# Linear attention feeding an ELU expert layer, one core: the first batch's queries and the first expert chunk cut into token halves, with a new order of the work

## The chip, the core and the metric

The kernel runs on one core of a Trainium2 chip. The core has five engines with a queue each: TensorE (PE, matrix products and transposes), VectorE (DVE), ScalarE (ACT), GpSimd (POOL) and SyncE (SP, which here only starts transfers). Products land in PSUM, which has eight banks. The metric is the time of one launch in microseconds (us), the median over several runs.

## The reference

For eight batches of eight heads with 576 tokens of 64 values, `q` and `k` go through a feature map: a product with `w_phi` (64 x 128), less the largest absolute value of the row, then the exponential of it and of its negative. Linear attention follows, and its output, heads joined to 512 values a token, goes through two products with an ELU between them.

```python
def phi(x):
    proj = np.einsum('bhsd,df->bhsf', x, w_phi)
    proj = proj - np.max(np.abs(proj), axis=-1, keepdims=True)
    return np.concatenate([np.exp(proj), np.exp(-proj)], axis=-1)
q_p, k_p = (phi(q), phi(k))
kv = np.einsum('bhsf,bhsd->bhfd', k_p, v)
z = np.sum(k_p, axis=2)
num = np.einsum('bhsf,bhfd->bhsd', q_p, kv)
den = np.einsum('bhsf,bhf->bhs', q_p, z)[..., None] + 1e-06
x = (num / den)            # then (4608 tokens) x (512 values)
h = x @ w_in               # 512 -> 2048
g = np.where(h > 0.0, h, np.exp(np.minimum(h, 0.0)) - 1.0)
out = g @ w_out            # 2048 -> 512
```

## The kernel before

**Tiles.** The attention goes by quads: quad i is four heads of batch i // 2, so there are 16. Each sequence of 576 tokens is four tiles of 128 and a tail of 64; the tails of two heads share a tile. The expert layer goes by chunks of 512 tokens: chunk b is the 512 main tokens of batch b and needs quads 2b and 2b + 1 both, since each gives half of the 512 values; chunk 8 is all the tails.

**A quad** (`plan_quad`), with the names that stand in the profile:
- keys and queries are transposed, for the first five quads by PE through PSUM (`tr`, and `trt` for tails; copied to `kT` and `qT` by DVE or ACT), later by transposing transfers on SP's queue;
- the feature products: `pk` (keys, and also queries in token-major form, for the maxima) and `pq` (queries in feature-major form);
- maxima by DVE (`m_k`, `m_q`), exponentials by ACT (`EK` with its tails `EKt`, `Eq` with its tails `Eqt`), the row scales from the maxima by ACT (`em` for keys, `w` for queries);
- the values times the key scales by POOL (`vs`), then `pkv` on PE and its copy `kv`;
- the outputs `pn` and `pnt` (tails) on PE, weighed with `w` and added by DVE into `tot`, a divide (`den`, `rec`), and the product `x`, by DVE for quads 0 and 1 and by POOL later;
- `x` transposed into `xT`, for the first four quads by PE and a copy, later by a transfer.

**A chunk** (`plan_chunk`): 16 feature tiles; for each four matmuls of 512 columns into one bank (`ph`), the exponential by ACT (`e_sb`), minus one by POOL (`u_sb`), and the ELU by DVE (`gT`), which frees the bank. Then for each of four token tiles 16 matmuls (`po`), a copy (`o_sb`) and a store.

**Order.** `Planner` lists all of this once, as operations with a cost for each engine that may take them, and plays it through in its own model of time: at each moment an engine takes, of the operations that can start, the one with the lowest rank. The ranks are a table written into the file (`RANKS`). What comes out is a fixed order of instructions for each engine; on the chip each engine runs its list in order and waits at semaphores. PSUM banks are given out by the same play: at most four `ph` and two `po` banks at once, and six for the attention once the first `ph` has begun. While PE stands idle in the model's first 60 us, matmuls of zeros into a spare bank (`fill`) are put into the gap. Transfers of inputs and weights are started from POOL's list (and `v` from batch 2 on from SP's), so they stand in line with POOL's arithmetic.

The waits of an output tile on the `x` of the quad before and the fill rule are these lines:

```python
[o, w, *quads.get(i - 1, {}).get("x", [])],
...
if e == "PE" and 0.0 < free[e] and now < self.FILL_UNTIL and banks:
    n = int(0.5 * (now - free[e]) / self.FILL)
    if n:
        if filled not in banks:
            filled = min(banks, key=banks.get)
        self.fill(filled, n)
```

Of the kernel before, what the change touches and what calls it, by code (L numbers as in the profile page):

```python
# [34 lines left out]
    "0E0H0I0O0Q0F0J0L1T1R2Q1U2X2k1S0K2n333B2W2a3R2OHR2Y3X4b1i0z0G3s3Y0y0n3S0p0r3V0s0q"  # L35
    "3U0w0o3W0x1M1N1Q0+0v3h2g2c2b2d2e2f0X0D0A0S0U11100Z3M3O1X1c2628491K1Z1Y1v0a070b0C"
    "Ai0Y05Ah0V047k0j007m0k01Ag0W061I1F1q6A4f1+3D7A2N2B6U9m4Z2U5R6W4k1j1A181h1P191o1C"
    "1B151716090u13120t1V1W2t2i2z2r2o2s2q0d0f0g1x1z1u1y1f02032J2H2I2L4A1e1O1D2K7y1d7i"
    "2x41366w466x39483A0-4U34824T7d9G2Z3v3E4N3q3Q524H2V3F407N74AF8g2h6-4C8W8z6m3Z6D8h"
    "7P2T9B14683f42575n4I449s5o5KC14w583JC64q5d6bCy4hAj7ID35y7K1ECN5v6d08Bl676Y4xBi5g"  # L40
    "5S4yDF5w4V4uBf4v6J6t6oBU3l9H8d8v986y6MAl6B8Y9ABc4D6TBXBZ7T80Dl2v6a0B1a692m3d3z4c"
    "72201n1t1J1p1r1G1w241H1l1m1L232925274B473K3L3N3H3T3P3I0c2-314O4Q4M530P323k4J4L55"
    "4K0i354X4a500m544e3w3r3m4i4oC7C52j434E2D4YB-4d4jBpD50N0M4m6NBwB63c6f1g1b4g2R813y"
    "0l4SC05C5A3n3u593o4+4-3x5B7583213+1s2271733i3a5M3b2M2P2S2C8b8a5W5V5s5T2A8X8Z6l6n"
    "6k6h0R30454W5r6H1-5F7+5z9K9T60A+Cb5ZCLBL64DKBo5aCs9U7H9v9w6j66AxA-6SBa8E7c9PE4EI"
    "CX6G6q9-8u788L6z5t7G4GA2CZ9L5iF8Cf9uAV5IDo8j95EPDh9XASEpEc9z8IF66e8F7wEi8T9D6PBN"
    "8RAIBQDx3eAYC89FL8BYBK6OGOEQ9RHMEa9yABBO9JEgDpAHExEs9IFlA0927o7W8xGwAD9SAJD2ChEW"
    "AM2+2u2w2y0T0h2l5699C42G5O6i7x4l655q7b7e5+7q7l5x7J7S5u7L7MCQ5L5P5Q5N7X7t9x6L6s6F"
    "6p6E6I3-5-625U5b5X5c519O9Q79776v764PDH5j5h6c6RBd6XAe4r9oEy5l9t5k7F9W634n8G9a7R9N"
    "5e614s4t7f7n973t3G0e5f5YBSAXA3AaA8A5BEBIAWAwAGAEBk8H8A8B879p9rGdEHEDEAGJEFGH5pD8"  # L50
    "DBATARAUAP6VFVFWBgCwBjBh5m90BH9lCdAAE37QDXECHwGNEBHIHyA1HlGGEEGMHzBJL7GCDZFpFoAO"
    "AQMz4FH68eBFFzDn84OHCpKE9cM5ApDQ9jLhDDKpAbOmGEFI8UL0BMGyGuDdW6DjWGCPB7AsDVFOCVB9"
    "7DFN8tE-EZ7uE58kG49gJjANK2CiVXDPEnGhWID0ACC3BTCnBzDrCMHaBRVVF+DgE7CmCuOdEMDbEKEN"
    "I5BAGKDCKvEtK5D4GR2p37383C888Q2F6+3p7O3j9VCY856r9b868N8y8K8O9Z8M898+7a8J7p7r7s7v"
    "DsD-DyDm9EE1Dz70DuDaCACGCECI6Q8S8PD7D6D9DA8D8-9493CJEGCoE9Bn91GFGPA9LMJY8wG6H17U"
    "GxIZ7CG+GT2EG9GABCEX1k4p4R6u7E7jHeC9CKHS8sCHHnBuCCHYCBBmHABBCtCTCRB+C2E+B1AkB4Af"
    "B2BG7YHhHjF2FMF4FL7VHqHtC-BsC+Bq7ZLrCWCaFKCx6ZCv6CB39d7zBDA79CBW8c8fLf9i9eB57-8m"
    "8VAqAvEUHmCeOqEjByCDK7F3NPFEOYGIOsDfW19+N4DWWMTLEmAmVxTGAdEJJUPnJ2KKMvLsFCG7EdE0"
    "G5HcCcHQJKH-H5DY6KImFYEYFSFTFaHkGnGLFFF-HpDcIcHUJfHbEwK4EkG2L1ItIsNYESIFI-IxJhGr"
    "F9IKJVIPJ0UbFPIeJrJTGqPRH43g8o4z8nALAK7g7hDq8CCg96MHOZOcMLLGIhLaIwJWLdJaOhGbCzCO"  # L60
    "BrD1JuLEKkKVKdJIKuL4KZCFNQNVO9O4LVLOCrONOUMbMkMYMm8l5J9h9fMuDRG8DSHGGBHLFxG1HOFd"
    "GDHKFwG0HPFvIlE2KbFQH0H2I3ER6gAZ7B9MBVCjJZWNWQJMWKWSJXWLWRJcWJW7WU5H5E5G5DW9W8TI"
    "WVV1V0THTEWZBPBtBvJoJpJvJsAtGZGXWDWCWAWFDtWHWPWOJkIkEVDeHsI0AoAzI1AnAyEq9kB8IjBe"
    "8rGfBbAuK3JqJnElFAH8NgKnPLFrOfLwMMHiJPEvP2H3O-KRPFGtO7JCPDHBIEGlJdMAIpI9MQLnGgH+"
    "OiLmGvIzNfLjIiOBMcLiPkHgN2LUPoNqIULqPbLZORLxPhMaKCMIQuI+NkNNOvKWN5KaLWNZNcHVMPIa"
    "L5NdNaK9HfKSVlLoQfNEKGKQQTPuQLRVJ8Gj8pNJ8qFtFuG3HCLyMTFHHoGWFnFkGQFhFeGaFcFmGUFb"
# [252 lines left out]
def kernel(  # L319
# [10 lines left out]
    nc = tc.nc  # L330
# [987 lines left out]
```

## Time and profile before

| what | value |
|---|---|
| time, median of 4 runs | 369.94 us (368.76 to 371.3) |
| the profiled execution: time and span | 368.76 us, 367.0 us |
| granted TensorE clock | 1.000 |
| read from memory, written | 36.77 MB, 9.44 MB |
| first `ph` matmul | 47.56 us |
| last PE instruction ends | about 363.2 us |
| fills | 179 |

Shares of busy time are averages over stages with different limits. For one stage, the busy time by stretches and the time line are read. In a time line line stand the start, the duration (from the first start to the last end of a merged run), the engine, the line of the kernel, the operation, output <- input, the shape, the count, and in brackets how long the engine was idle before it and what ended that. Durations of PE overlap, because matmuls are pipelined; the step from one start to the next is what one costs in a row. In the stretches, after each engine's busy time stands its count of instructions, and at the end the granted clock, the mean share of the 16 DMA engines and GB/s.

### The profile page before, as it was taken

The page shows a single profiled execution, that of the slowest core. Times are in us where ns is not written, and L with a number is a line of the kernel's source. Part 1 is how long each engine was busy: PE and PEld are TensorE (multiplying, and loading weights), DVE is VectorE, ACT ScalarE, POOL GpSimd, SP SyncE. Part 2 cuts the span into 40 slices and gives each one's busy share as a digit, 9 for nine tenths or more (in the row PEclk, how much of TensorE's full clock was granted, in tenths as well). Part 3 has the DMA queues.
Part 4 walks back from the last instruction along what each step waited for, and adds up shares of the span by engine and source line. Part 5 has one row for each costly group of instructions (what it writes and reads, how often), then busy time and mean ns, then how long its engine had stood idle before and what let it go on. Part 6 is the DMA issues. An engine that isn't in the chain of part 4 may idle for free.

```text
span 367.0 us, 8937 instructions
## 1 busy us (share of the span) xinstructions
PE 350.3 (95%) x3355; PEld 194.6 (53%) x3403; DVE 270.7 (74%) x568; ACT 268.3 (73%) x595; POOL 234.1 (64%) x333
## 2 busy tenths in 40 slices
PE   7887899999999999999999999999999999999995
PEld 6666655655555554455554554565446444444444
DVE  5898999888988878875777889799968751655120
ACT  2999996899898877995669979877787623555321
POOL 8895878769795687487649573947593742545210
PEclk9999999999999999999999999999999999999999
DMA  7999999991869989578855128583210113000113
GB/s 134 238 238 205 197 198 165 175 159 51 172 142 113 129 208 193 143 144 118 102 96 153 31 40 192 149 191 67 57 63 30 35 37 109 4 29 28 59 29 86
DMA packets 86651, 43.18 MB, mean 118 GB/s; under 512 B 55632, under 2 KB 80592, under 8 KB 86608
## 3 DMA queue, kind: packets, MB, share of 16 engines
q1 hardware_dynamic: 57360, 26.36, 33.2%
q0 software_dynamic: 28848, 15.73, 30.9%
q8 instruction: 26, 0.43, 0.5%
q10 hardware_dynamic: 400, 0.52, 0.4%
q14 instruction: 17, 0.14, 0.2%
HBM read 36.77 MB, written 9.44 MB: 126 GB/s over the span
## 4 chain that ended last, share of the span: by engine, by line
PE 74%; ACT 7%; POOL 5%; DMA 4%; DVE 4%; issue 3%; SPq 1%; POOLq 0%; DVEq 0%; ACTq 0%
PE po L1128 30%; PE ph L1062 27%; PE pk L608 4%; PE pkv L828 4%; PE pn L881 3%; POOL vs L713 3%; ACT EK L659 2%; DMA v_b<-in_v_dram 2%; ACT Eq L796 2%; DMA xT<-x 1%; PE pq L746 1%; ACT EKt L659 1%; DMA k_b<-in_k_dram 1%; POOL u_sb L1078 1%; POOL x L959 1%
## 5 line engine op out<-in xcount | busy, mean ns | idle before, releaser
L1078 POOL TENSOR_SCALAR u_sb<-e_sb 128x512 bf16<-128x512 f32 x144 | 88.1, 617 | 74.2 <-ACT e_sb L1074 67.2
L1128 PE MATMUL po<-w_out_sb,gT 128*128 128x512 bf16 (+1 forms) x570 | 132.7, 373 | 1.6 <-issue 1.0
L1085 DVE SCALAR_TENSOR_TENSOR gT<-u_sb,ph 128x512 bf16<-128x512 bf16 x144 | 96.7, 681 | 46.7 <-POOL u_sb L1078 46.1
L1062 PE MATMUL ph<-xT,w_in_sb 128*128 128x512 bf16 x486 | 120.0, 379 | 1.9 <-DVE gT L1085 0.4
L1074 ACT ACTIVATE e_sb<-ph 128x512 f32<-128x512 f32 x144 | 86.1, 609 | 40.5 <-PE ph L1062 36.6
L1128 PEld LDWEIGHTS <-gT 128*128 128x128 bf16 x592 | 54.4, 98 | 57.5 <-issue 2.9
L1062 PEld LDWEIGHTS <-w_in_sb 128*128 128x128 bf16 x576 | 53.0, 98 | 60.1 <-issue 4.1
L713 POOL TENSOR_TENSOR vs<-v_b,em 128x512 bf16<-128x512 f32 (+1 forms) x96 | 77.9, 840 | 1.0 <-DMA v_b<-in_v_dram 0.9
L659 ACT ACTIVATE EK<-pk 128x512 bf16<-128x512 f32 x128 | 67.2, 622 | 12.3 <-PE pk L608 12.2
L796 ACT ACTIVATE Eq<-pq 128x512 bf16<-128x512 f32 x128 | 68.3, 623 | 6.4 <-PE pq L746 6.1
L626 DVE TENSOR_REDUCE m_q<-pk 128x4 f32<-128x512 f32 (+1 forms) x80 | 47.4, 626 | 9.5 <-PE pk L608 8.2
L626 DVE TENSOR_REDUCE m_k<-pk 128x4 f32<-128x512 f32 (+1 forms) x80 | 47.5, 628 | 8.9 <-PE pk L608 5.4
L959 POOL TENSOR_TENSOR x<-tot,rec 128x576 bf16<-128x576 f32 x28 | 31.7, 1151 | 18.8 <-DVE rec L955 18.6
L1151 ACT COPY o_sb<-po 128x512 f32<-128x512 f32 (+1 forms) x23 | 13.1, 568 | 30.1 <-PE po L1128 29.8
L916 DVE TENSOR_TENSOR tot<-pn,w 128x260 f32<-128x260 f32 x64 | 26.4, 421 | 2.2 <-PE pn L881 1.7
L881 PEld LDWEIGHTS <-Eq 128*128 128x128 bf16 x512 | 22.2, 97 | 8.9 <-issue 0.3
L922 DVE TENSOR_TENSOR tot<-tot,pn 128x260 f32<-128x260 f32 x64 | 25.9, 418 | 0.4
L828 PE MATMUL pkv<-vs,EK 128*128 128x65 bf16 x512 | 24.5, 194 | 1.2 <-POOL vs L713 0.9
L828 PEld LDWEIGHTS <-EK 128*128 128x128 bf16 x512 | 22.2, 98 | 6.3 <-issue 2.0
L881 PE MATMUL pn<-kv,Eq 128*128 128x65 bf16 x512 | 25.1, 194 | 0.1
L659 ACT ACTIVATE EKt<-pk 64x256 bf16<-64x256 f32 x64 | 22.9, 378 | 1.7 <-PE pk L590 1.1
L828 PE MATMUL pkv<-vs,EKt 128*128 128x65 bf16 x128 | 21.2, 193 | 0.8 <-POOL vs L713 0.8
(73 smaller groups left out, 289.3 us busy)
## 6 DMA issues: line engine op xcount, KB each, us to landing
out_dram<-o_sb SPq DMA_DIRECT2D x32, 256.0 KB, 2.6
v_b<-in_v_dram SPq DMA_DIRECT2D x6, 1024.0 KB, 6.4
k_b<-in_k_dram POOLq DMA_DIRECT2D x7, 512.0 KB, 7.6
q_b<-in_q_dram POOLq DMA_DIRECT2D x7, 512.0 KB, 11.3
w_in_sb<-in_moe_w_in_dram POOLq DMA_DIRECT2D x2, 1024.0 KB, 18.2
w_out_sb<-in_moe_w_out_dram POOLq DMA_DIRECT2D x4, 512.0 KB, 16.9
v_b<-in_v_dram SPq DMA_DIRECT2D x32, 32.0 KB, 5.2
v_b<-in_v_dram POOLq DMA_DIRECT2D x2, 512.0 KB, 9.5
```

The costliest lines, as they stand in the source:

```text
L626: nc.vector.tensor_reduce(dst, src, axis=AX.X, op=ALU.max, apply_absolute_value=True)
L659: nc.scalar.activation(EK()[:, 2 * c + par, sg, :] if c < 2 else EKt[r, s, sg, :], bank.tile[r, 0:n, :].rearrange("p a b -> p (a b)"), ACT ...
L713: nc.gpsimd.tensor_tensor(st["vs"][:, sg].rearrange("p (c n) d -> p c n d", c=2)[:, :, r, 0:D], kqv[b, 2][:, o:o + 2 * n * D].rearrange("p ...
L796: nc.scalar.activation(dst, src, ACT.Exp, scale=1.0 - 2.0 * sg)
L828: nc.tensor.matmul(pkv[:, c, sg, :], st["EK"][:, 2 * s + t % 2, sg, (2 * c + t // 2) * F:(2 * c + t // 2 + 1) * F,] if t < NT else EKt[:, ...
L881: nc.tensor.matmul(pt[:, t, :], st["Eq"][:, par, s, sg, o:o + P], st["kv"][:, s, c, sg, :], start=True, stop=True,)
L959: (nc.vector if e == "DVE" else nc.gpsimd).tensor_tensor(tile("x", work, [P, NS, 2, D], BF16)[:, :, c, :], tot[:, r, 0:D], st["rec"][:, r, ...
L1062: nc.tensor.matmul(ph, w_in_sb[:, ct, jt * P:(jt + 1) * P], xTs[ch][:, ct, :] if ch < B else xT_tail[:, ct // 2, :, ct % 2, :], start=(ct ...
L1074: nc.scalar.activation(t["e"], bank.tile, ACT.Exp)
L1078: nc.gpsimd.tensor_scalar(t["u"], t["e"], -1.0, 1.0, op0=ALU.add, op1=ALU.mult)
L1085: nc.vector.scalar_tensor_tensor(gTs[ch][:, jt, :], t["u"], 0.0, bank.tile, op0=ALU.min, op1=ALU.max)
L1128: nc.tensor.matmul(bank.tile, gTs[ch][:, jt, tt * P:(tt + 1) * P], w_out_sb[:, jt, o0:o1], start=(jt == 0), stop=(jt == N_JT - 1),)
```

## The change

For batch 0 (quads 0 and 1):
- the two query groups of a quad are no longer the head pairs but the token pairs: group c takes tiles c, c + 2, c + 4, c + 6 of `qT` (a strided read), that is both head pairs for half the tokens. The outputs, weights `w`, divides, products `x`, transposes and copies into `xT` follow by halves (and tails by themselves), each waiting only for its half.

For chunk 0:
- a `ph` bank holds two feature tiles of 256 tokens instead of one of 512. The first half of the matmuls of a bank needs only quad 0's half of `xT`, the second only quad 1's; all of the first token half comes before the second. `po` of the first two token tiles needs only the first half's `gT`.

For the planner:
- fills go only into a bank that has been free as long as PE, and are counted from the later of the two; 41 fills stand at the start instead of 30; the list of ranks is new throughout, so the order of every engine changes, and of the loads too: the first transfer is of `q` and not of `k`.

The core of the diff (the new `half_` functions hold the same arithmetic as the old ones on half the tokens):

```diff
-                    n = int(0.5 * (now - free[e]) / self.FILL)
-                    if n:
-                        if filled not in banks:
-                            filled = min(banks, key=banks.get)
+                    if filled not in banks or banks[filled] > free[e]:
+                        filled = min(banks, key=banks.get)
+                    n = int(0.5 * (now - max(free[e], banks[filled])) / self.FILL)
+                    if n > 0:
                         self.fill(filled, n)
...
+        halves = b == 0
...
-                project_halves(1, c, pair)
+                blocks = slice(c, 8, 2) if halves else slice(4 * c, 4 * c + 4)
+                project_halves(1, range(8)[blocks], pair)
...
-        w = add({"ACT": 0.12}, weights, m_q, key=-3.0)
+        if halves:
+            w_ops = [
+                add({"ACT": 0.12}, lambda e, tp=tp: weights_of(e, tp), m_qs[tp], key=-3.0)
+                for tp in range(3)
+            ]
+        else:
+            w_ops = [add({"ACT": 0.12}, weights, m_q, key=-3.0)] * 3
...
+            def half_outputs(e, tp=s, s=c, pair=pair):
+                for sg in range(2):
+                    pt = psum(pair[sg], [P, NT, D1], FP32, f"pn{sg}")
+                    for c in range(2):
+                        for par in range(2):
+                            o = (2 * s + c) * P
+                            nc.tensor.matmul(
+                                pt[:, 2 * c + par, :],
+                                st["Eq"][:, par, tp, sg, o:o + P],
+                                st["kv"][:, s, c, sg, :],
+                                start=True,
+                                stop=True,
+                            )
...
-            copies = kv_copies if hh == 4 else [kv_copies[s]]
-            exps = Eq_ops[s]
+            copies = kv_copies if hh == 4 else [kv_copies[c if halves else s]]
+            exps, w = Eq_ops[s], w_ops[s]
+            last = quads.get(i - 1, {})
+            last_x = last["x_ops"][s] if i == 1 else last.get("x", [])
...
-                [o, w, *quads.get(i - 1, {}).get("x", [])],
+                [o, w, *last_x],
...
+            for tp in range(3):
+                div = add(
+                    {"DVE": 0.3 if tp < 2 else 0.25},
+                    lambda e, tp=tp: divide_half(e, tp),
+                    tot_ops[tp],
+                    key=-9.0,
+                )
+                for c in range(2 if tp < 2 else 1):
+                    x_ops[tp].append(
+                        add(
+                            {"DVE": 0.36 if tp < 2 else 0.2},
+                            lambda e, tp=tp, c=c: x_half(e, tp, c),
...
-        for jt in range(N_JT):
+        for step in range(N_JT):
+            hf, jt = divmod(2 * step, N_JT) if ch == 0 else (0, step)
...
+            def mm1_half(e, g, hf=hf, jt=jt, bank=bank):
+                if g == 0:
+                    psum(bank, [P, 2, CHUNK // 2], FP32, "ph")
+                for j in range(2):
+                    for ct in (2 * g, 2 * g + 1):
+                        nc.tensor.matmul(
+                            bank.tile[:, j, :],
+                            w_in_sb[:, ct, (jt + j) * P:(jt + j + 1) * P],
+                            xTs[ch][:, ct, hf * CHUNK // 2:(hf + 1) * CHUNK // 2],
+                            start=(j == 0 and ct == 0),
+                            stop=(j == 1 and ct == N_CT - 1),
+                        )
...
+            if ch == 0:
+                for g in range(2):
+                    o = add(
+                        {"PE": 0.44},
+                        lambda e, g=g, f=mm1_half: f(e, g),
+                        [quads[g]["xT"][hf], landed["w_in", jt // 8]]
+                        + ([o] if g else []),
...
-                    [g_ops[jt] for jt in jts]
+                    [
+                        g_ops[jt if n_half == 1 else tt // 2 * 8 + jt // 2]
+                        for jt in jts[::n_half]
+                    ]
...
-    fill(7, 30)
+    fill(7, 41)
```

## The prediction

> **What bounds the kernel now.** I read the page's first two parts first, then the busy time by stretches, then the time line of the first 60 us engine by engine.
>
> ```profile
> PE 350.3 (95%) x3355; PEld 194.6 (53%) x3403; DVE 270.7 (74%) x568; ACT 268.3 (73%) x595; POOL 234.1 (64%) x333
> ...
> PE   7887899999999999999999999999999999999995
> ...
> DVE  5898999888988878875777889799968751655120
> ACT  2999996899898877995669979877787623555321
> ```
>
> TensorE (PE) is the bound of the whole, but the first five slices are thinner, and there ACT and DVE are as full as PE. The stretches before and after the first expert matmul say more:
>
> ```profile
> 0.00:47.56 47.56, 39.22 (x633) 31.53 (x634) 39.26 (x89) 39.34 (x97) 37.84 (x54) 1.00 1.23 202
> 47.56:60.00 12.44, 12.34 (x109) 6.34 (x108) 11.88 (x26) 10.86 (x24) 9.85 (x16) 1.00 1.41 174
> 60.00:363.30 303.30, 298.73 (x2621) 156.71 (x2665) 219.52 (x456) 217.72 (x475) 186.36 (x264) 1.00 0.54 103
> ```
>
> From 47.56 us PE idles 4.7 us in all. Before that its 39.2 busy us are pipelined durations, with 179 fills that compute nothing. Counted by the step from one start to the next, PE's own work there is 80 transposes x 0.0565 + 18 tail transposes x 0.075 + 112 narrow `pk` x 0.0345 + 8 wide `pk` x 0.108 + 12 `pq` x 0.155 + 8 tail `pq` x 0.055 + 216 matmuls of 65 columns x 0.0315 = 19.7 us. So 28 us of the ramp are not PE's. Only there can this change gain much, and every us by which PE reaches the same work sooner is a us of the total, as long as nothing stops PE later.
>
> ```profile
> 32.19 1.28 PE L1281 MATMUL fill<-zeros 128*128 128x128 bf16 x20 [1.65 <-DVE m_k L626]
> 34.32 0.61 PE L1011 MATMUL tr<-ident,x 128*128 128x128 bf16 x8
> ...
> 44.44 0.19 PE L828 MATMUL pkv<-vs,EKt 128*128 128x65 bf16 x1 [0.78 <-POOL vs L713]
> ...
> 45.91 0.61 PE L1011 MATMUL tr<-ident,x 128*128 128x128 bf16 x8
> ...
> 47.56 1.02 PE L1062 MATMUL ph<-xT,w_in_sb 128*128 128x512 bf16 x3
> ```
>
> The gate of the first expert matmul is the second transpose of `x` (quad 1, 45.91), and in front of it PE stands in order behind quad 2's `pkv`, which waits for GpSimd's `vs`. Quad 1's `x` itself was ready at 44.1:
>
> ```profile
> 13.79 3.54 ACT L659 ACTIVATE EK<-pk 128x512 bf16<-128x512 f32 x7 [0.31 <-PE pk L608]
> ...
> 43.32 0.80 DVE L959 TENSOR_TENSOR x<-tot,rec 128x576 bf16<-128x576 f32 x1
> ...
> 59.14 0.60 ACT L1074 ACTIVATE e_sb<-ph 128x512 f32<-128x512 f32 x1 [1.17 <-PE ph L1062]
> ```
>
> Seven exponentials in 3.54 us give ACT's step, 0.483. Until 59.14 ACT has hardly a gap.
>
> **The change part by part.** All sums are made on the profiled execution: 368.76 us, of which 367.0 are span; the median of the runs is 369.94, 1.2 higher.
>
> *When does the expert flow start?* In the instruction lists of the two programs I look for the point at which the changed PE has done as much of its own work as the old one at 47.56. That is the second half of the first `ph` tile: before it lie 84 transposes (4.7), 17 tail transposes (1.3), 88 + 7 `pk` (3.0 + 0.8), 10 + 6 `pq` (1.6 + 0.3), 200 narrow matmuls (6.3) and 16 half `ph` of 256 columns at half of 0.216 (1.7): 19.7 us as well. It needs ACT's copy of quad 1's first half of `xT`. Three chains lead there:
> - ACT: up to that copy 44 exponentials x 0.483, 16 `EKt` x 0.33, 4 `Eqt` x 0.265, 12 small ones x 0.11, 3 `kv` x 0.27, 5 tail copies x 0.16, 2 copies of 1024 x 0.91, 2 half copies x 0.483 = 33.3 us. It starts at 8.4 (8.2 now). Without idle time that is 41.7. The old list reached 33.5 us of work at 43.1 with 1.4 idle, and 38.4 at 48.8 with 2.2 idle. Ends: 41.8 and 44.0; I take 1.3 idle, the nearest row: 43.0.
> - DVE: 29.8 us of work up to quad 1's first half of `x` (22 reductions x 0.60, 14 `tot` steps, 7 large copies, the rest small), from 6.8: 36.6. The old list had 32.5 us up to its `x` and 4.7 idle. With as much, 41.3; transposes 0.45 and copy 0.5: 42.3.
> - POOL: quad 2's scales come after 26.0 us of ACT (35.2 with 0.8 idle), six `vs` take 4.8 (the row at 23.85), `pkv` 0.6, transposes 0.45, copy 0.5: 41.6.
>
> So 43.0 against 47.56: 4.5 us earlier, with the queue order that put `pkv` in front still there but ending sooner.
>
> *What halves cost.* Queries by token halves change no count of exponentials or reductions. For the two quads the divides become 6 of each kind instead of 2, the `x` products 10 instead of 4, the DVE copies of `xT` 2 instead of 1. The divide's two lines are
>
> ```profile
> 29.06 0.19 DVE L954 TENSOR_REDUCE den<-tot 128x18 f32<-128x36 f32 x1
> 29.29 0.27 DVE L955 RECIPROCAL rec<-den 128x18 f32<-128x18 f32 x1
> ```
>
> By starts, `tot` of 260 elements steps 0.335 and of 130 elements 0.20, so one more instruction costs 0.065 plus its elements; 15 more cost 1.0 us at least, and 2.2 us with the divides at 0.42 each, which I take. It is inside the 29.8. DVE is not the last of the three chains, so it costs nothing there while those 0.7 us of slack hold; without them it costs up to 2.2. [...] ACT gains four `w` (0.44) and a split copy (0.06), inside the 33.3.
>
> *The first four tiles.* From the start of flow PE has 4.5 us of work until `po` needs the fourth pair's `gT`: 47.5. DVE has 7.5 us from quad 1's first `x` (40.8) to that `gT`, 4 x 0.595 of it the ELUs: 48.3. PE waits about 0.8; with the first `gT` also freeing the bank for the fifth `ph`, I take 1.0 (ends 0 and 2.5, if DVE idles as it did). Behind PE's wait stand `ph` 5 and quad 3's `pk`. For the next four pairs ACT has 10.4 us to the last exponential (53.4), POOL 0.58 and DVE 0.6 behind it: 54.6, while PE gets there at about 56.4. No wait.
>
> *Fills.* 129 instead of 179. The old ones waited 1.65 us for a bank at 32.19 and 0.5 at 23.47; that goes, but mostly into the waits for ACT and DVE already counted, so nothing for itself. The 11 more at the start end at about 0.99 + 41 x 0.11 = 5.5, before the first data at 5.76: free. Granted clock is 1.00 in every stretch, with idle gaps up to 1.65 us. [...]
>
> *Loads.* Half the expert's input weights (`w_in`, second half) move behind quad 0's `vs` on POOL:
>
> ```profile
> L385 POOL DMA_DIRECT2D w_in_sb<-in_moe_w_in_dram x1: 778/778/778, 21.0 to 21.0; - x1
> ...
> DMA to landing us min/median/max: 19.4/19.4/19.4
> ```
>
> The new issue comes after second scales at 18.7, 4.8 of `vs` and the issue itself: 24.4, landing 43.8; the fifth pair asks at about 46. Covered by 2 us, beyond that one for one. On SP the first output store now stands ahead of quad 5's query transposes and the next `v`: `v` is issued at about 62.7 instead of 57.0 and lands 10.8 later, at 73.5; quad 4's `vs`, at 79.2 now, would ask at 75.7. Covered too, and its keys are not the next chunk's gate.
>
> *Sum.* 4.5 - 1.0 = 3.5 us. After 60 us both programs hold the same work, and chunk order is alike; I add nothing for the new ranks there and leave 1 us either way. 368.76 - 3.5 = 365.3 for a profiled execution, 369.94 - 3.5 = 366.4 for the median. Ends: 41.8 with no stall and 0.6 better later, 363.6; 44.0 with 2.5 of stall and 1 us worse later, 369.8.
>
> **Rivals.** *Given back* (no change): DVE is the true limit of the ramp. Up to the reciprocal of quad 2 the lists hold 49.25 us of DVE work after and 49.28 before, with 9 and 10 ELUs in it. If DVE idles 6.6 us again, that reciprocal stays at 62.5, and all that is left is what PE has done by then: about 36 us against 34.7, less what it waits later, 0.7 net: 369.2. For it: DVE is 95% busy from 47.56 to 60. Against: its old gaps were waits for PE and POOL in other places. *Weights late* (slower): the second half of `w_in` lands after 46, and PE, in order, stops at the fifth pair. Four POOL waits before DMA issues add to 5.3 us in the old ramp; if all fell ahead of this issue, and 0.5 MB more in front of it took 2.5 us at 0.206 MB/us, it would land at 51.6: 5.6 us of stall, 2.1 us slower, 372.0. It is slower than before from a landing at 49.5. Against: the loads that those issues wait for are earlier ones. *Fills or halves not in force*: excluded, the program's lists show both.
>
> **How the numbers follow.** The forecast 0.62, given back 0.25, weights late 0.13. About 0.5% (1.85 us) is what a measurement of this kernel can tell from no change; the forecast's own range (363.6 to 369.8) crosses that bound at its upper end, and I count that part with "given back". The range reaches from 363.6 to 371.2, into the third case, and leaves out about 2 in 10.
>
> **What would show it.** Right: `xT` copy of quad 1's first half by ACT ending near 43, a first `po` near 47, the reciprocal of quad 2 near 59 to 60, PE idle after 60 us below 6. Wrong: first `po` after 51 (weights, in the DMA line of `w_in`), DVE idle over 6 us before quad 2's reciprocal, or PE waits after 60 us that were not there.

## The result, and the profile after

The changed kernel takes 371.81 us (median of 43 runs, 369.56 to 374.17), the kernel before in the same runs 370.28 (64 runs): ratio 1.0042, 95% interval 1.0031 to 1.0053. The forecast was 366.4, in a range that ended at 371.2. The change is slower by about 1.5 us, which is still inside the 0.5% that I had set as "no change", but it lost where I had counted 3.5 us won.

The first two parts of the page of the changed kernel, the same lines as before and the clock:

```profile
PE 350.2 (95%) x3369; PEld 200.7 (54%) x3417; DVE 276.5 (75%) x583; ACT 269.3 (73%) x600; POOL 232.7 (63%) x333
...
PE   7766899999999999999999999999999999999995
...
DVE  5869899897989989786887987689988763533500
ACT  2995899899998897996679796998984553544411
...
PEclk9986799999999999999999999999999999999999
```

PE's first five slices read 77668 instead of 78878, and the clock, which was 9 throughout, falls to 8, 6 and 7 in the third to fifth. By stretches, cut at the point that the prediction worked with (the `ph` run at which PE has done what it had done at 47.56 before):

```profile
0.00:49.80 49.80, 37.42 (x553) 31.16 (x554) 40.12 (x87) 36.24 (x89) 35.31 (x52) 0.86 1.24 206
49.80:60.00 10.20, 9.79 (x98) 6.83 (x97) 9.99 (x25) 9.26 (x22) 5.20 (x8) 1.00 1.23 141
60.00:366.70 306.70, 303.00 (x2724) 162.72 (x2769) 226.37 (x473) 223.44 (x490) 192.23 (x273) 1.00 0.53 102
```

The point lies at 49.80, 2.2 us later than before, where 43.0 was predicted. From it to the end of the span it is 320.6 us against 319.4, so 1.2 us more, where the prediction had 1.0. 2.2 + 1.2 = 3.4 is the whole difference of the two spans (370.4 and 367.0). The medians differ by 1.5 only: the profiled execution of the kernel before, 368.76, is the fastest of its 64 and lies 1.5 under their median, that of the changed kernel, 372.22, lies 0.4 above its own. Measured on these two executions, as the prediction's sums were, all that went wrong lies ahead of the point.

The time line there, all engines, has one line that does not belong (the first group of each line is start and duration):

```profile
30.22 0.17 DVE L1051 RECIPROCAL rec<-den 128x2 f32<-128x2 f32 x1
...
30.40 3.06 POOL L724 TENSOR_TENSOR vs<-v_b,em 128x512 bf16<-128x512 f32 x3
...
30.62 3.00 DVE L1069 TENSOR_TENSOR x<-tot,rec 128x128 bf16<-128x128 f32 x1
33.40 0.94 POOL L411 DMA_DIRECT2D q_b<-in_q_dram  x1
...
33.68 0.29 PE L1140 MATMUL trt<-ident,x 128*128 128x128 bf16 x1 [2.76 <-DVE x L1069]
...
34.00 0.27 ACT L1148 COPY xT_tail<-trt 128x128 bf16<-128x128 bf16 x1 [2.78 <-PE trt L1140]
```

A product of 128 elements, 0.28 us where no `vs` runs (at 34.22 in the run e1 below), is on DVE for 3.00 us. It ends 0.2 us after the third of three `vs` on GpSimd. PE stands 2.76 us for it, and ACT 2.78 us behind PE. Busy time hides this: DVE counts as busy, and is even busier than before (75% against 74%).

### The profile page after: what moved, and what is told of

Same layout as the page of the kernel before. It is cut to its first block, busy times and chain, and to the rows that moved or that the text cites. A ratio compares the mean times of both kernels' runs of the same rounds, so it can differ in the third digit from the quotient of the medians.

```text
span 370.4 us, 8987 instructions
## 1 busy us (share of the span) xinstructions
PE 350.2 (95%) x3369; PEld 200.7 (54%) x3417; DVE 276.5 (75%) x583; ACT 269.3 (73%) x600; POOL 232.7 (63%) x333
## 4 chain that ended last, share of the span: by engine, by line
PE 71%; DVE 9%; POOL 8%; DMA 4%; issue 4%; ACT 3%; POOLq 0%; ACTq 0%
PE po L1338 31%; PE ph L1236 21%; PE pkv L858 5%; PE pk L609 4%; PE pn L912 3%; POOL u_sb L1268 3%; PE ph L1251 3%; DMA t_b<-in_k_dram 2%; POOL vs L724 2%; DVE x L1069 2%; DVE gT L1280 2%; DMA out_dram<-o_sb 2%; POOL x L1030 2%; PE pq L760 1%; DVE m_k L637 1%
## 5 line engine op out<-in xcount | busy, mean ns | idle before, releaser
L1264 ACT ACTIVATE e_sb<-ph 128x512 f32<-128x512 f32 x144 | 86.5, 612 | 40.1 <-PE ph L1236 37.1
L1236 PE MATMUL ph<-xT,w_in_sb 128*128 128x512 bf16 x426 | 104.0, 379 | 1.2
L1236 PEld LDWEIGHTS <-w_in_sb 128*128 128x128 bf16 x512 | 47.7, 98 | 52.6 <-issue 1.5
L670 ACT ACTIVATE EK<-pk 128x512 bf16<-128x512 f32 x128 | 68.2, 634 | 2.4 <-PE pk L609 1.6
L858 PEld LDWEIGHTS <-EK 128*128 128x128 bf16 x512 | 23.6, 101 | 7.6 <-ACT Eq L811 2.6
L858 PE MATMUL pkv<-vs,EK 128*128 128x65 bf16 x512 | 25.5, 199 | 2.3 <-ACT Eq L811 2.1
L971 DVE TENSOR_TENSOR tot<-pn,w 128x260 f32<-128x260 f32 x56 | 23.0, 422 | 5.5 <-PE pn L912 5.0
L912 PEld LDWEIGHTS <-Eq 128*128 128x128 bf16 x448 | 19.1, 97 | 7.5
L977 DVE TENSOR_TENSOR tot<-tot,pn 128x260 f32<-128x260 f32 x56 | 22.7, 418 | 0.4
L858 PE MATMUL pkv<-vs,EKt 128*128 128x65 bf16 x128 | 22.2, 198 | 0.0
L912 PE MATMUL pn<-kv,Eq 128*128 128x65 bf16 x448 | 21.1, 194 | 0.1
```

Source lines behind the costliest of these rows:

```text
L670: nc.scalar.activation(EK()[:, 2 * c + par, sg, :] if c < 2 else EKt[r, s, sg, :], bank.tile[r, 0:n, :].rearrange("p a b -> p (a b)"), ACT ...
L858: nc.tensor.matmul(pkv[:, c, sg, :], st["EK"][:, 2 * s + t % 2, sg, (2 * c + t // 2) * F:(2 * c + t // 2 + 1) * F,] if t < NT else EKt[:, ...
L912: nc.tensor.matmul(pt[:, t, :], st["Eq"][:, par, s, sg, o:o + P], st["kv"][:, s, c, sg, :], start=True, stop=True,)
L1236: nc.tensor.matmul(ph, w_in_sb[:, ct, jt * P:(jt + 1) * P], xTs[ch][:, ct, :] if ch < B else xT_tail[:, ct // 2, :, ct % 2, :], start=(ct ...
L1264: nc.scalar.activation(t["e"], flat(bank.tile), ACT.Exp)
```

## The experiments

Three theories. *Port*: DVE products and sums of two operands in SBUF (where the kernel keeps its tiles that are not PSUM banks) wait while GpSimd runs `vs`; the name is my guess at the cause, which no run shows. *Clock*: fewer fills let the granted clock fall (0.61 from 30 to 40 us), and PE's slow matmuls make the ramp late. *Count*: the 15 more DVE instructions by themselves. The table shows for each run the longest wait found on DVE (the duration of the instruction that has it), the granted clock from 20 to 30 and 30 to 40 us, the point, the rest of the span after it, and the median with its ratio to the kernel before on the same chip.

| kernel | longest on DVE, us | clock | point | rest | median | ratio |
|---|---|---|---|---|---|---|
| changed | `x` 3.00 | 0.83, 0.61 | 49.80 | 320.6 | 371.81 | 1.0042 |
| e1 old fills | `den` 2.73 | 0.83, 1.00 | 49.43 | 321.6 | 372.64 | 1.0064 |
| e2 tail of `x` on ACT | `den` 3.31 | 0.83, 0.59 | 49.44 | 320.8 | 371.48 | 1.0018 |
| e3 both | `den` 2.52 | 0.83, 0.83 | 51.36 | 320.7 | 372.67 | 1.0077 |
| e5 e2 and `den` by reduction | `x` 2.48 | 0.83, 0.68 | 46.90 | 320.8 | 369.09 | 0.9982 |
| e6 e5 and old fills | `x` 1.83 | 0.83, 1.00 | 47.77 | 320.7 | 371.05 | 1.0020 |
| e7 e5, first `x` on ACT | none; 2.48 for ACT | 0.83, 0.69 | 47.43 | 320.8 | 370.72 | 1.0002 |
| e8 quad 1's `vs` cut | `den` 4.54 | 1.00, 0.81 | 48.95 | 320.9 | 371.76 | 1.0030 |
| e11 e8 and `den` by reduction | `x` 3.33 | 1.00, 0.75 | 48.83 | 320.7 | 371.21 | 1.0011 |
| e12 e11, quad 2's `vs` cut | `x` 3.33 | 1.00, 0.70 | 47.70 | 320.8 | 370.25 | 0.9995 |
| e13 `x` by scalar products | `x` 3.79, 3.57 | 1.00, 0.66 | 51.95 | 321.2 | 376.43 | 1.0163 |
| e14 e13 and old fills | `x` 2.65 | 0.83, 0.77 | 54.69 | 321.4 | 377.23 | 1.0162 |
| e17 e5, `x` between `m_k` | `x` 1.08 | 0.83, 0.83 | 45.52 | 320.9 | 368.66 | 0.9940 |
| e18 e17 without later fills | `x` 1.30 | 0.68, 0.66 | 46.33 | 320.9 | 368.53 | 0.9935 |

The rest is 320.6 to 321.6 us in all of them: what such a profiled execution takes is settled by when it arrives at the point. e4, e9, e10, e15 and e16, whose order is another, stand in the text.

**e1 to e4: fills, or the tail of `x`.** e1 puts the old fill rule and `fill(7, 30)` into the changed kernel, e4 the new rule and `fill(7, 41)` into the kernel before. e2 computes the tail of `x` on ACT, e3 is e1 and e2.

```diff
...
-                rec = rec[:, :, NS - 1, None].to_broadcast((P, 2, D))
+                for h in range(2):
+                    nc.scalar.activation(x[:, NS - 1, h, :], z[:, h, NS - 1, 0:D],
+                                         ACT.Copy, scale=rec[:, h, NS - 1:NS])
...
```

> The changed kernel with the fill rule and the 30 opening fills of the kernel before (30 opening fills in place of 41, and a fill group wherever PE waited in the plan, counted from the end of PE's last work, not only in banks long free); every other instruction keeps its place. Clock theory (fewer fills let the granted clock fall to 0.6 between 25.6 and 43 us, and that made the ramp late): clock 1.00 in every stretch, the first po some 1.5 to 3 us before 54.15, the time 1.5 to 3 us below that of the changed kernel, 371.8, so 369 to 370.3. Port theory (DVE's product x of two SBUF inputs waits for GpSimd's vs): the product of 128 elements still takes about 3 us, PE still waits some 2.7 us for it, quad 2's scales stay near 39, and the time stays within 0.7 us of 371.8, whatever the clock. Count theory (the 15 more DVE instructions by themselves): 371.8 within 0.5.

> The changed kernel with the tail part of x (128 elements, two of them in the program) computed by ACT, as two copies of 64 elements with rec as scale, at the same place of the plan; the fills stay as they are. Port theory: no 3 us instruction on DVE, PE's wait of 2.76 us before the tail transpose falls below 1 us, quad 2's scales come 2 to 2.5 us before 39.7, the first po before 52.3, the time 1.5 to 2.5 us below 371.8, so 369.3 to 370.3. Clock theory: the clock still falls to about 0.6 and the time stays within 0.7 us of 371.8. Count theory: two DVE instructions fewer and two on ACT, 371.8 within 0.5.

> Both edits together: the old fills and the tail part of x on ACT. If clock and port are both causes and add: the sum of the gains of the two single edits, 3 to 4.5 us below 371.8, so 367.3 to 368.8, below the kernel before (370.3), first po at 50 to 51. Port theory alone: as the run with only the tail on ACT, within 0.5. Clock theory alone: as the run with only the old fills, within 0.5. Count theory: 371.8 within 0.7.

> The kernel before with only the new fill rule and 41 opening fills; no other instruction moves. Clock theory: with fewer fills the clock falls in this order of work too (below 0.9 in some stretch between 15 and 47 us) and the time rises by 1 us or more above 370.3. If the fall of the clock needs the new order (its gap of 1.89 us before 24.65, or the 2.76 us behind the 3 us product): clock 1.00 throughout and 370.3 within 0.5. Port theory says nothing else than 370.3 within 0.5.

Neither edit helped (e1 1.0064, interval 1.0031 to 1.0097; e2 1.0018, 0.9995 to 1.0041; e3 1.0077, 1.0050 to 1.0104), and the count theory alone would have said so too. But both time lines show why. e1 has the clock back at 1.00 from 30 us on, and DVE still stands:

```profile
31.04 2.73 DVE L1050 TENSOR_TENSOR den<-tot 128x2 f32<-128x2 f32 x1
```

Here it is `den` that waits; the tail product behind it takes 0.28. In e2, whose tail product is no longer on DVE, the DVE line and GpSimd's are:

```profile
29.08 3.31 DVE L1050 TENSOR_TENSOR den<-tot 128x2 f32<-128x2 f32 x1
...
29.30 3.06 POOL L724 TENSOR_TENSOR vs<-v_b,em 128x512 bf16<-128x512 f32 x3
```

The wait moved to the sum just before it: an addition of two elements for each partition, 3.31 us. I had expected it to vanish and had overlooked that `den` too has two SBUF operands in the changed kernel (in the kernel before it is a reduction of one). e4 has the new fills in the old order. In its time line the fills that stood in the gap are gone:

```profile
32.40 0.41 PE L896 MATMUL pnt<-kv,Eqt 128*128 128x65 bf16 x8 [1.66 <-DVE m_k L626]
33.79 1.01 PE L1011 MATMUL tr<-ident,x 128*128 128x128 bf16 x8 [0.99 <-ACT EK L659]
```

Eight transposes take 1.01 us instead of 0.61: the clock is at 0.50 from about 33.8 to 37 us. Still the point that starts the flow (first `ph`) is at 47.4 instead of 47.6 and the span 367.0 as before. So the clock falls with the new fills in the old order too, as the clock theory said, and in this execution no time follows. Over the runs the ratio is 1.0025 (0.9992 to 1.0058), which leaves it open: of the 11 executions compared five took 368.7 to 369.8 us at a mean clock of 0.991 to 0.995, the other six 371.2 to 373.7 at 0.982 to 0.990. The profiled one is among the five. What the six lost, and whether the lower clock is its cause or its trace, no profile shows.

**e5, e6: no two-operand `den`.** To e2, all `den` of batch 0 come by a reduction of one operand (e6 adds the old fills).

```diff
...
-            nc.vector.tensor_tensor(den, z[0], z[1], op=ALU.add)
+            nc.vector.tensor_reduce(den, z, axis=AX.X, op=ALU.add)
...
```

> The changed kernel with the tail part of x on ACT and all of batch 0's denominators den summed by a reduction over one SBUF operand, as in the kernel before, in place of an addition of two SBUF operands; fills as in the changed kernel. With the tail of x on ACT alone the wait had only moved: the addition of 2 elements took 3.31 us beside three vs. Port theory: the reduction beside the same three vs takes 0.2 us, PE's wait of 3 us before the tail transpose falls below 1 us, quad 2's second scale comes at 36.5 to 37.5 instead of 39.7, the first po at 51 to 52 instead of 54.15, the time 2 to 3 us below 371.8, so 368.8 to 369.8. Rival (whatever DVE gains, quad 2's scales and PE wait for something else, ACT's list or a load): the 3 us wait goes, but the scales stay after 38.5 and the time stays within 0.7 us of 371.8. If DVE waits for GpSimd whatever its operands are, the reduction too takes 2 us or more.

> The kernel with den by reduction and the tail of x on ACT, and the old fill rule with 30 opening fills besides. The old fills alone brought the clock from 0.61 to 1.00 between 30 and 40 us and moved no time (372.6). Clock theory in its weaker form (the clock counts once the port wait no longer covers it): clock 1.00 from 30 us on, first po 0.5 to 1.5 us before that of the run with the new fills, 367.5 to 369. Without it: as the run with the new fills, within 0.5, or up to 1 us worse where the fills themselves wait for a bank.

The time line of DVE in e5:

```profile
29.13 0.15 DVE L1050 TENSOR_REDUCE den<-tot 128x2 f32<-128x4 f32 x1
...
29.84 0.17 DVE L1050 TENSOR_REDUCE den<-tot 128x8 f32<-128x16 f32 x1
...
30.46 2.48 DVE L1069 TENSOR_TENSOR x<-tot,rec 128x256 bf16<-128x256 f32 x1
```

The second reduction runs in 0.17 us while GpSimd's three `vs` run (29.58 to 32.6), so DVE does not wait for GpSimd as such. The next product of two operands takes the wait over. It now stands behind the tail transpose, PE gets on at once, and the point comes 2.9 us earlier than in the changed kernel: 369.09 us, ratio 0.9982 (0.9964 to 1.0000). DVE has as many instructions as in e2 (581), and the point comes 2.5 us earlier than there, so the count theory is out as the main cause. With the old fills (e6) the clock is 1.00 from 30 us on and the time 371.05 (1.0020): the weaker clock theory (the clock counts once the wait is gone) fails as well, as far as fills can test it. In e6 a group of PE's fills waits for a bank that ACT still reads (at 24.45, 1.78 us of idle time that ends with ACT's `Eq`), and quad 1's scales come 1.2 us later than in e5.

**e7 to e10: the rest of the wait, its length, the halves, the old order.** e7 puts quad 0's first half of `x` on ACT too (8 copies of 64 elements). e8 leaves DVE alone and cuts quad 1's four large `vs` in two. e9 undoes the gate by halves. e10 gives the kernel before a two-operand `den`.

```diff
e8
+            for c in range(2) if s < 2 and i == 1 else [slice(0, 2)]: nc.gpsimd.tensor_tensor(
...
e9
-                        [quads[g]["xT"][hf], landed["w_in", jt // 8]]
+                        [*quads[g]["xT"][hf:], quads[1]["xT"][1], landed["w_in", jt // 8]]
e10
-            nc.vector.tensor_reduce(den, tot[:, :, D:], axis=AX.X, op=ALU.add)
+            nc.vector.tensor_tensor(den, tot[:, :, D], tot[:, :, D + 1], op=ALU.add)
```

> The kernel with den by reduction and the tail of x on ACT, and besides quad 0's first half of x (two products of 256 elements, of which the first took 2.48 us beside the three vs) as eight copies of 64 elements on ACT, with rec as scale. Port theory: no DVE instruction between 28 and 38 us is longer than 0.8 us, quad 2's second scale comes at 35.3 to 36.2 (the prediction of the blind sum was 35.2) instead of 37.5, the first po at 49 to 50 instead of 50.7, the time 1 to 2 us below the 369.1 of that kernel, so 367 to 368, a clear gain on the kernel before. Rival (ACT is the limit by now; eight more copies cost it 0.9 to 1.3 us in front of quad 2's exponentials): the scales stay at 37 or later and the time within 0.7 us of 369.1 or above. If the wait moves again, another product of two SBUF operands of over 1.5 us shows it.

> The changed kernel with quad 1's four large vs on GpSimd each cut into two of 256 elements; DVE's list is untouched. It asks how long the wait is. If DVE waits until the running GpSimd instruction ends: the tail product of x takes at most 0.8 us in place of 3.00, PE's wait of 2.76 us falls below 1 us, the time 1.5 to 2.5 us below 371.8. If it waits until GpSimd's run of queued instructions ends: it still takes 2.5 to 3.5 us and the time stays at 371.8 within 0.7, or 0.3 us above for the longer run. If it waits for two or three instructions: 1.2 to 2 us and about 1 us less.

> The changed kernel with chunk 0's halves undone in one respect: every first-layer tile of chunk 0 waits in the plan for all four transposed copies xT of the two quads, not only for those of its own 256 tokens; all else is as in the changed kernel, but the planner puts other work in front. What the token halves buy by themselves: if they are worth what the blind sum said (the flow starts 4.5 us earlier, 3.5 of it kept), this kernel is 1.5 to 3.5 us slower than 371.8, so 373.3 to 375.3. If the halves buy little, because the second halves of xT come only 3 to 5 us after the first and PE has other work to do: 371.8 within 0.8. If the halves themselves cost (more small matmuls, more waits): faster than 371.

> The kernel before with one edit: its 16 denominators den by an addition of two SBUF operands in place of a reduction of one (0.18 us each, none above 0.19); every instruction keeps its place. Port theory: where GpSimd has no tensor instruction running (29.06) it stays at 0.2 us; beside vs, u or x on GpSimd it waits, so that several of the 16 take 0.5 to 3 us and the longest lies beside a run of vs; the time rises by 0.3 to 2 us above 370.1, as far as DVE's list is on the path. Rival (the 3 us of the changed kernel are special to it, a late semaphore or the tail's layout): all 16 at 0.15 to 0.25 us, 370.1 within 0.5.

e7 went the rival's way. The wait beside `vs` is gone and another has its place and its length (DVE's time line):

```profile
34.59 2.37 DVE L637 TENSOR_REDUCE m_k<-pk 128x2 f32<-128x256 f32 x4 [2.48 <-ACT EKt L670]
```

ACT's copies stand in front of the `EKt` that PE's banks wait for. 370.72 us, 1.0002.

e8, time line of DVE and GpSimd:

```profile
30.41 0.50 DVE L1068 TENSOR_TENSOR x<-tot,rec 128x256 bf16<-128x256 f32 x1
...
35.72 4.78 POOL L724 TENSOR_TENSOR vs<-v_b,em 128x128 bf16<-128x128 f32 x6
35.98 4.54 DVE L1049 TENSOR_TENSOR den<-tot 128x8 f32<-128x8 f32 x1
```

Beside quad 1's cut `vs` the products run almost unhindered, quad 2's scales come at 34.5 (35.2 predicted, 39.7 in the changed kernel), and then an addition of eight elements waits through all six of quad 2's `vs`. The gain of the one place is lost in the other (1.0030; 1.0009 to 1.0050). e11 shows that the cut is no cure: there a product waits 3.33 us beside cut `vs`. So the wait can last to the end of GpSimd's run, three to six instructions, or less than one (0.6 to 0.8 us for `den` and `x` at 41.2 to 45.6 in the changed kernel). What decides which, the runs do not tell.

e9: 375.6 us, 1.0152 (1.0126 to 1.0178), 3.8 us above the changed kernel, with the order planned anew around the later gate. As far as a newly planned order can price it, the halves are worth about what they were counted at. The 3 us wait is in this kernel too (`x`, 3.07 us at 29.54).

e10: the 16 `den` of the old order,

```profile
L954 DVE TENSOR_TENSOR den<-tot x16: 181/188/902, 29.0 to 300.1; 128x18 f32<-128x18 f32 x16
```

have a median of 0.188 us, but five of them take 0.49 to 0.90. The longest, at 231.27, lies beside a run of `vs`, the other four beside `u` (minus one, on GpSimd), and each of these four ends within 0.05 us of GpSimd's instruction. Two lines of that time line:

```profile
184.02 0.62 POOL L1078 TENSOR_SCALAR u_sb<-e_sb 128x512 bf16<-128x512 f32 x1 [1.23 <-ACT e_sb L1074]
184.07 0.60 DVE L954 TENSOR_TENSOR den<-tot 128x18 f32<-128x18 f32 x1
```

So the wait is nothing special to the new order, nor to `vs`. The time is hardly touched: the ratio is 1.0013 (0.9997 to 1.0030), less than the port theory expected; in the old order `den` falls only once beside a run of `vs`, and late. The edit that is costly in the new order is nearly free in the old.

**e11, e12: cut `vs` and reduced `den`.** e11 is e8 with the reduction; e12 cuts quad 2's `vs` as well (`i in (1, 2)`).

> The changed kernel with quad 1's four large vs cut in two (which took the 3.00 us of the tail's x to 0.28 us and quad 2's second scale to 34.5, where the blind sum had 35.2, but let the addition of 8 elements beside quad 2's uncut vs wait 4.54 us) and with all of batch 0's den by reduction of one SBUF operand, so that this addition is gone too. Port theory: no DVE instruction between 27 and 45 us above 1.3 us, first po at 49 to 50.5 in place of 53.3 with the cut alone, time 367.3 to 369, below the kernel before (370.3). Rival (ACT is the limit once the port is free): first po after 51 and 369.5 or more, ACT without gaps from 20 to 50 us. If the wait moves to a product x beside quad 2's vs: one x of 2 to 4.5 us near 36.5, and 370.5 to 371.5.

> The same with quad 2's four large vs cut as well, which makes GpSimd's list longer by four steps of about 0.13 us before quad 2's pkv. Port theory: as the run with one quad cut where that run shows no wait on x beside quad 2's vs, but up to 0.5 us later for the longer list; where that run does show one, this one is free of it and 1 to 3 us faster: first po at 49.5 to 50.5, 367.5 to 369. Rival (ACT is the limit): both within 0.5 us of each other and at 369.5 or more.

Both keep one wait of 3.33 us (`x`, quad 0, beside quad 1's cut run). In e11:

```profile
31.84 3.33 DVE L1068 TENSOR_TENSOR x<-tot,rec 128x256 bf16<-128x256 f32 x1
```

The ratios are 1.0011 (0.9988 to 1.0033) and 0.9995 (0.9974 to 1.0016).

**e13, e14: `x` with one SBUF tensor.** Every `x` of batch 0 as products of one tensor with a scalar of each partition (e14 with the old fills); `den` by reduction.

```diff
-            nc.vector.tensor_tensor(dst, z, rec, op=ALU.mult)
+            for j in range(4 if tp < 2 else 2):
+                k = (slice(None), j // 2, j % 2) if tp < 2 else (slice(None), j)
+                nc.vector.tensor_scalar(dst[k], z[k], rec[k][:, 0:1], None, op0=ALU.mult)
```

> The changed kernel with every den of batch 0 by reduction and every x of batch 0 by products of one SBUF tensor with a scalar of each partition (tensor_scalar, two or four instructions of 64 elements where one product of two tensors stood: 36 in place of 10), all still on DVE at the same place; GpSimd's list and ACT's are untouched. Port theory in its narrow form (only DVE instructions with two SBUF tensors wait): no DVE instruction from 27 to 45 us over 0.8 us, quad 2's second scale at 35 to 36, first po at 49 to 50, 367.2 to 368.8, some 3 to 4 us below the changed kernel. If a product with a scalar of the partition waits for GpSimd too: one such instruction of 2 to 4 us near 30 and 370.5 to 372. Rival (with the port out of the way ACT or the added DVE instructions, 26 x 0.06 = 1.6 us, hold the ramp): no long instruction, but the scales at 37 or later, first po after 51, 369.5 or more.

> The same with the old fill rule and 30 opening fills. It asks what the clock is worth once the port wait is gone. Clock theory: the clock is below 0.85 between 24 and 42 us with the new fills and 1.00 from 30 us on with these, first po 0.5 to 1.5 us earlier, the time as much lower. Otherwise: within 0.5 us of the run with the new fills, or up to 2 us above it, as in the earlier pair (369.1 and 371.1), because fills that wait for a bank stand in front of PE's own work.

The narrow form was wrong: these wait as well, twice (DVE's time line in e13):

```profile
28.88 3.79 DVE L1071 TENSOR_SCALAR x<-tot,rec 128x64 bf16<-128x64 f32 x2
...
40.84 3.57 DVE L1071 TENSOR_SCALAR x<-tot,rec 128x64 bf16<-128x64 f32 x4
```

Alone two such take 0.4 and four 0.73 us. The two waits, 3.4 and 2.8 us, replace one of 2.7 and smaller ones, and 26 more instructions stand in DVE's list. The time rises to 376.43, 4.6 above the changed kernel. e14 is 377.23, the same ratio (1.0162) at a clock of 0.77 instead of 0.66.

**e15, e16: `x` behind quad 2's `m_k`, planned anew.** `x` (in e16 without the tail) gets quad 2's `m_k` as predecessors; the planner then orders all that follows differently.

```diff
...
+    for o in quads[0]["x_ops"][2] + quads[0]["x_ops"][0]: o.behind += quads[2]["m_k"]
```

> The changed kernel with den by reduction and quad 0's tail and first half of x put behind quad 2's five m_k in DVE's list (an order that the planner is made to keep; what follows is planned anew, so later work moves too). x then runs at 34 us, when GpSimd's run of vs is nearly over. Port theory: no wait of over 1.3 us on DVE from 27 to 36 us, quad 2's second scale at 35 to 36 (39.7 in the changed kernel, 35.2 in the blind sum), first po at 49 to 51 if no new wait on x beside quad 2's vs takes its place, 367.5 to 369.5. If the later, newly planned order is worse, the scales come early all the same and the loss shows behind them. Rival (ACT or PE holds quad 2's scales): 38 or later.

> The same, with the tail of x on ACT at its old place and only the first half of x behind quad 2's m_k. Port theory: scales at 35 to 36.5, first po at 49 to 51, 367.5 to 369.5; it keeps PE's order around the tail transpose. Rival (ACT holds the ramp): scales at 38 or later, 370 or more. Between this and the former: whichever has no x beside quad 2's vs from 37 to 42 us is faster by the length of that wait.

e15: 370.87 us, 1.0009 (0.9991 to 1.0027); two products `x` take 3.08 us at 41.98 (0.75 unhindered). e16 reaches its first `po` at 48.7 with the clock at 1.00 from 10 to 70 us, and takes 382.02 (1.0298): in the new plan PE idles 2.3 us from 85 to 95 us at a clock of 0.67, and more after. A new plan is another kernel; these two say little on the cause.

**e17, e18: the same lists, one move.** e17 is e5, in which quad 0's first half of `x` is issued after three of quad 2's five `m_k` on DVE; PE, ACT, GpSimd and SP keep their lists. e18 drops the 88 fills that the rule sets after the start.

```diff
+            if (i, tp) == (0, 0) and not st.get("go"): return st.setdefault("late", []).append(lambda: x_half(e, tp, c))
...
+            if (i, n, st["n"]) == (2, 0, 3):
+                quads[0]["st"]["go"] = True
+                for f in quads[0]["st"]["late"]: f()
```

> The kernel with den by reduction and the tail of x on ACT (369.1), and of that kernel only DVE's list changed in one place: quad 0's first half of x (two products, the first of which waited 2.48 us) stands behind three of quad 2's five m_k; the plan and the lists of PE, ACT, GpSimd and SP are the same. x then asks for the port at about 32.1, where GpSimd's run of vs ends at 32.6. Port theory: the two products take 0.4 to 1 us each, no wait over 1 us from 27 to 38 us, quad 2's second scale at 35.3 to 36.3 in place of 37.5, the first po at 49 to 50 in place of 50.7, 367.5 to 368.5, a gain of 0.5 to 0.8% on the kernel before. Rival (ACT holds quad 2's scales from here): 37 or later and 369 or more.

> The same without the 88 fills that the rule sets in the ramp (the 41 at the start stay). Clock theory: the clock is low for longer than with the fills, under 0.7 from 20 to 45 us, and each stretch of PE work that is waited for takes up to twice as long: first po 1 to 3 us later, the time as much above that run. If the clock in the ramp is worth nothing: the clock as low, the time within 0.5 us of that run or below, since fills also stand in front of PE's own work.

Time lines of e17 (DVE, ACT, PE):

```profile
33.43 0.95 DVE L1074 TENSOR_TENSOR x<-tot,rec 128x256 bf16<-128x256 f32 x2
```

```profile
36.47 0.34 ACT L705 ACTIVATE em<-m_k 128x18 f32<-128x18 f32 x2
```

```profile
45.52 1.47 PE L1256 MATMUL ph<-xT,w_in_sb 128*128 128x256 bf16 x12
```

Two products in 0.95 us (0.75 unhindered), scales at 36.5, the point at 45.52, the first `po` at 49.3. 368.66 us, 0.9940 (0.9914 to 0.9965): faster than both kernels, by the two ratios 1.0% under the changed one. Even here the products beside quad 2's `vs` take 1.08 and 1.00 instead of 0.41.

e18 in stretches:

```profile
15.00:40.00 25.00, 18.05 (x245) 13.57 (x244) 20.33 (x46) 22.36 (x62) 18.89 (x27) 0.64 1.28 223
```

A clock of 0.64 for 25 us, and 368.53 us, 0.9935 (0.9910 to 0.9960). In the two profiled executions the point is 0.8 us later without the fills; in the medians nothing is left of it. Fills and clock change together here, as in e1, e4 and e6: what is shown is that a higher clock bought with fills gained nothing, not what the clock alone would be worth.

## Why the prediction was wrong

*Where the flow starts (43.0): wrong by 6.8 us, and on the profiled execution this is all of the error* (372.22 against 365.3; between the measured median and the forecast it is 5.4 us). Three readings of that step; they overlap and are not to be added:
- The 15 more DVE instructions and the products `x` were costed at the steps that they have alone, as if a DVE instruction could only wait for its inputs. Beside `vs` they wait for GpSimd. To quad 2's scales that is 3.00 - 0.28 = 2.7 us; beside quad 2's `vs`, `den` 0.97 instead of 0.16 and two `x` of 0.98 and 0.99 instead of 0.41 add 1.95. Together 4.7 us. DVE's chain shows them whole: it ended quad 1's first half of `x` at 48.17 instead of 41.3, and from its first copy at 6.98 to there it is busy 35.4 us instead of the 29.8 counted, idle 5.8 instead of 4.7. (Of the 5.6 more, 4.7 are these waits; the last 0.9 is how I counted, by steps, which in the old list up to its `x` is 0.95 less than busy time.) That this wait is the cause of most of the loss is shown: it follows the operand form (a reduction beside the three `vs` 0.17, a sum 3.31), and with most of it moved out of the way in e17 the point comes 4.3 us earlier.
- ACT's list was given 1.3 us of idle time, "the nearest row", from the old order. Its copy of `xT` ended at 49.57 instead of 43.0. In the 41.21 us from its first exponential to there it is idle 6.26 us, of which 2.78 is the line shown above, and busy 34.95 instead of 33.3. Idle time is a property of an order; it cannot be carried over to a new one.
- Some 0.9 us were lost before: quad 1's scales came at 27.3 instead of 26.4. In e17 they came at 26.1, so that much differs between executions whose lists are the same up to there. POOL's chain left out an issue, `k_b` at 19.23 for 0.88 us, in front of quad 0's `vs`: the issue of `w_in` followed at 25.00 instead of 24.4.

*"DVE is not the last of the three chains, so it costs nothing"* is the sentence that failed, and so did the 2.2 us that it allowed at most without the slack: DVE's waits alone are 4.7. The change replaced the reduction `den` by a two-operand sum, which the description of the change leaves out and for which the prediction showed the reduction's line (0.19), and it spread ten products over the ramp, just where GpSimd now has its `vs`. The trace of before had the hint: DVE's `x` took 0.76 at 29.59 and 0.75 at 32.39, with GpSimd only starting transfers, and 0.96 and 0.80 at 40.63 and 43.32, beside `vs`. DVE's lines and GpSimd's:

```profile
29.59 0.76 DVE L959 TENSOR_TENSOR x<-tot,rec 128x576 bf16<-128x576 f32 x1
...
39.58 5.81 POOL L713 TENSOR_TENSOR vs<-v_b,em 128x512 bf16<-128x512 f32 x6
40.63 0.96 DVE L959 TENSOR_TENSOR x<-tot,rec 128x576 bf16<-128x576 f32 x1
```

I read the durations and not what ran beside them. Which forms wait, the runs show: sums and products of two SBUF operands (3.00 us in the changed kernel, 3.31 in e2, 4.54 in e8, 0.49 to 0.90 in e10) and products with a scalar of the partition (3.79 and 3.57 in e13), but not a reduction (0.17 in e5). On how long they differ: in e10 the four waits beside `u` end with the one instruction of GpSimd, to within 0.05 us; those beside `vs` do not, 3.00, 3.31 and 4.54 us are runs of three to six `vs` of 0.4 to 1.0 us each. Why DVE waits for GpSimd at all, no run shows.

*Fills: what they do for the clock was missed, the weight given to them was about right.* From the gaps of up to 1.65 us in the kernel before, at a clock of 1.00, I took it that the clock stays at 1.00 with fewer fills too. It fell to 0.50 after gaps of 1.89 us (changed kernel, from 25.5 us on) and of 1.66 and 0.99 (e4). (In the kernel before, a gap of 1.65 us with 20 fills behind it left the clock at 1.00.) But it cost little: e1, e4, e6 and e18 change fills and clock in the ramp, between 0.6 and 1.0, and none shows a measurable gain for the higher clock.

*After the point: the number came near, its reason did not.* 1.0 us was taken, for PE waiting on the fourth pair's `gT`, and 1.2 measured. But PE's longest wait for a `gT` there is 0.36 us, and from the point to its end PE is idle 4.1 us in all, against 4.7 before. The stretch is longer because PE is busy longer, 312.8 us against 311.1; why is not traced. That the two numbers agree is luck. The second half of `w_in` never stopped PE: the weights rival did not occur. On SP, `v` went out at 75.5 and not at 62.7, and quad 4's `vs`, at 86.5, did not have to wait for it. Quad 2's reciprocal came at 69.4, not 59 to 60.

*The mechanism of the halves: probably right, not isolated.* e9 puts their gate at 3.8 us (4.5 less 1.0 predicted), though with another order behind it, and e17, free of most of the wait, has 1.9 to 2.2 us of gain over the kernel before instead of 3.5.

*Given back* named DVE as the limit but by the length of its list. It was the limit by a wait that the list does not show. Two of the signs that I had named for being wrong came: the first `po` at 54.15, though no weights were waited for, and DVE idle for some 7 us before quad 2's reciprocal. Neither points at the wait, which counts as busy. What stays open: why DVE sometimes gets in after less than one `vs` and sometimes only after the whole run, and the last 1 us or so of e17's distance to the predicted point, beyond the 1.3 us of its waits beside quad 2's `vs`.

## What to carry to other kernels

When an order changes, list for each two-operand sum or product and each scalar product on DVE what GpSimd runs at that moment; a product that took 0.28 us alone took 3.00 here, and what stood behind it in order waited with it, PE for 2.76 us and ACT for 2.78. Read a duration together with what stood beside it, and look for instructions whose duration does not fit their size: a wait of this kind counts as busy time and does not appear in the list of DVE's waits (in the changed kernel, from 20 to 60 us, it has 3.4 us, all before `kv`, `m_k`, `qT` and `kT`). If one such instruction is taken away, the next one can inherit the wait (3.31 us in e2, 2.48 in e5); move the consumers that matter (here `m_k`) in front of it instead.

## What the runs showed of the hardware that I had not expected

- An addition of two elements for each partition on DVE lasted 3.31 us, one of eight 4.54 us, beside GpSimd's `vs`; a reduction of one operand beside the same three `vs` 0.17 us. Beside GpSimd's `u` an addition of 18 elements lasted 0.49 to 0.63 instead of 0.18 us.
- Products with a scalar of the partition (64 elements, float32 to bfloat16) waited as well: 3.79 us for two, which alone take 0.4, and 3.57 for four, which alone take 0.73.
- The granted clock fell to 0.50 after idle gaps of 1.89 us (changed kernel) and of 1.66 and 0.99 us (e4), in stretches with few fills, and a ramp of 25 us at 0.64, with 88 fills fewer, cost no measurable time (368.53 us in e18, 368.66 in e17).
